# Sparse attention and a two-layer MLP on one core: batches 2 to 7 loaded by casting DMAs, MLP chunks one after the other, attention steps placed by a written plan

## The chip, the core and the metric

One NeuronCore of a Trainium2 chip runs the whole program. Its engines are TensorE (PE, with PEld for weight loads), VectorE (DVE), ScalarE (ACT), GpSimd (POOL) and SyncE (SP, which here only issues DMAs). The metric is the device time of one execution in microseconds.

## What is computed

Eight batches with eight heads of 576 tokens and 64 features go through masked attention, and the result, 4608 tokens by 512 features, through a two-layer MLP with a squared ReLU. Heads 0 to 3 are local (a key is seen if it lies 0 to 31 positions back), heads 4 to 7 are strided (a key is seen if it is not later and has the same position modulo 32).

```python
scores = scale * np.matmul(q, k.transpose(0, 1, 3, 2))
rel = pos[:, None] - pos[None, :]
mask_local = (rel >= 0) & (rel < 32)
mask_strided = (rel >= 0) & (pos[None, :] % 32 == pos[:, None] % 32)
attn = softmax(np.where(masks, scores, -1e9))
x = np.matmul(attn, v)            # then to (4608, 512): heads side by side
h = x @ w_in                      # 512 x 2048
g = np.maximum(h, 0.0) ** 2
out = g @ w_out                   # 2048 x 512
```

## The kernel before

**Units.** A unit is a pair of heads of one batch. Unit u = 4b + p: p = 0, 1 are the local pairs of batch b, p = 2, 3 its strided pairs; so units 4 to 7 are batch 1, units 8 to 11 batch 2, and so on. A local unit has six blocks of 96 queries with 128 keys each, a strided unit eight blocks of 72 queries with 72 keys.

**Steps of a unit.** T (`step_T`, L270) transposes rows of q or k by six or eight PE transposes (L278) into a PSUM bank and copies it to SBUF on ACT (q, L291) or DVE (k, L293). S (`step_S`, L299) computes the scores (L327), four exponentials on ACT (L337, a half of one head each) and two mask products on DVE (L343); for units above 3 the exponentials and masks are handed out one per group by `later`. D (`step_D`, L385) multiplies with v (L405) in two or three parts and normalizes on DVE (L417, L418). E (`step_E`, L421) brings the result into `xt`, the MLP's input with features on partitions: by PE transposes (L435) and a copy (L441, L443), or, for local units from batch 2 on, by a DMA transpose (L428). For strided units of batch 0 the steps N and O (L359, L372) take the place of D and E: row sums by a product with ones, 1/sum by Ln and Exp on ACT, and the product with v straight in the layout of `xt`.

**Loads.** Batches 0 and 1 come largely by casting DMAs that POOL issues (float32 in HBM, bf16 in SBUF). From batch 2 on, SP loads float32 rows of q, k (L111, L117) and v (L191, L235), and POOL casts them: q and k on L139, local v on L198 and, for the 32 keys ahead of each block, L199, strided v on L242. Strided q and k go from HBM to HBM with a cast (L159) and are read back by a DMA transpose (L167). Local q and k of batches 2 and 3 are transposed on PE (`has_T`, L521, with LB = 4), those of batches 4 to 7 by DMA transposes on SP (L179).

**MLP.** The 4608 tokens form nine chunks of 512. Chunk c needs `xt` of all batches up to c (chunk 8 needs no more than batch 7). The first layer of a chunk has 16 groups (`mm1`, L451): four matmuls of 512 columns (L459) into one of the two banks "ph", ReLU on ACT (L465), square on DVE (L466). The second layer has 16 groups (`mm2`, L470): four matmuls (L480), four groups to a bank, then a copy on ACT (L484) and a store issued by SP (L488). There are 288 groups in one list, and PE executes in the order in which instructions were written.

**What sets the order.** Chunks 0, 1 and 2 have their first and second layers one after the other, with the second layer of chunk 2 and all later ones interleaved, group by group, with the first layer of the next chunk (L692 to L697); the second layer of chunk 8 stands alone at the end. Batch 0 is written out by hand (`first_steps`, L505), batch 1 too (`second`, L727 to L746, groups 12 to 31), and from batch 2 on `stream_steps` (L524) makes one list of steps, which is dealt out over the groups in proportion to weights (L750 to L757). Loads of a batch hang on a group too (`plan`, L706). In the first 32 groups three groups (`NP`) of chunk 0 are done piecewise while the last units of batch 0 finish.

Of the kernel before, what the change touches and what calls it, by code (L numbers as in the profile page):

```python
# [11 lines left out]
ALU = mybir.AluOpType  # L12

@with_exitstack
def kernel(
# [16 lines left out]
    QL = 96  # L32
# [10 lines left out]
    qkT = ctx.enter_context(tc.tile_pool(name="qkT", bufs=3))  # L43
# [28 lines left out]
    mask_loc = singles.tile([128, 1, QL], BF16)  # L72
    mask_str = singles.tile([SP_, 1, SP_], BF16)
# [3 lines left out]
    vl_sts = [singles.tile([128, 2 * NL, D], FP32, name=f"vl_st{i}") for i in range(2)]  # L77
# [13 lines left out]
    rv0 = b0[:, n_s:n_s + 4 * S].bitcast(FP32).rearrange("p (u c) -> p u c", u=2)  # L91
# [10 lines left out]
    LB = 4  # L102

    def load_qk_local(u, eng, gate=None):
        b, p = units[u]
        s = st.setdefault(u, {})
        for name, src in (("q", q), ("k", k)):
            t = qk_st.tile([QL, 2, 6 * D], FP32, name=f"{name}_st")
            if b >= LB:
                for hh in range(2):  # L110
                    eng.dma_start(out=t[:, hh].rearrange("p (t d) -> p t d", d=D),  # L111
                                  in_=src[b, 2 * p + hh].rearrange("(t p) d -> p t d", p=QL))
                s[name + "f"] = t
                continue
            if gate is not None and name == "q":
                nc.gpsimd.tensor_copy(t[0:1, 0, 0:1], gate)
            eng.dma_start(out=t, in_=src[b, 2 * p:2 * p + 2]  # L117
                          .rearrange("h (p j) d -> p h (j d)", j=6))
            s[name + "f"] = t

# [12 lines left out]
    def cast_qk_local(u, copies, names="qk"):  # L133
        s = st[u]
        for name, copy in zip("qk", copies):
            if name not in names:
                continue
            t = qk_in.tile([QL, 6, 2, D], BF16, name=f"{name}_l")
            copy(t.rearrange("p j h d -> p h j d"),  # L139
                 s[name + "f"].rearrange("p h (j d) -> p h j d", j=6))  # L140
            s[name] = t

    def load_qk_str(u):
        b, p = units[u]
        s = st.setdefault(u, {})
        for name, src in (("q", q), ("k", k)):
            t = strT.tile([128, NJ // 2, 4 * SP_], BF16, name=f"{name}T_s")
# [75 lines left out]
    def load_str_first(names):  # L223
        for i, (name, src) in enumerate((("q", q), ("k", k))):
            if name not in names:
                continue
# [572 lines left out]
```

## Time and profile before

| what | value |
| --- | --- |
| three runs | 321.79, 324.76 and 327.16 us, median 324.76 us |
| profiled execution | span 320.8 us, granted clock 0.999; no time of its own is recorded beside the span |
| matmuls of the first layer, L459 | 561 of 576 recorded |
| mean of one ReLU (L465), of one exponential (L337) | 597 ns, 406 ns |
| mean of one square (L466) | 486 ns |
| POOL casts and copies L139, L198, L199, L221, L242 | 820 to 1780 ns each |

The span runs from the first to the last instruction. In the chain of waits each piece is what the end of the program waited for at that moment; "issue" is time in which nothing visible was waited for. In a row of the timeline the first number is the start in microseconds, the second the duration, and the bracket says what the engine sat idle for.

### The profile page before, as it was taken

The numbers are of one execution on the slowest core, as the hardware profiler recorded it, in microseconds if no ns is written. First come the engines' busy times: TensorE is split into PE (matmuls) and PEld (weight loads), VectorE is DVE, ScalarE is ACT, GpSimd is POOL, SyncE is SP. The second block draws the span as 40 slices with busy tenths as digits, with TensorE's granted clock in tenths as the row PEclk, the third lists the DMA queues.
The fourth block names the chain that finished last, engine by engine and source line by source line (L and its number), as shares of the span: only waits on it lengthen the run. The fifth ranks groups of instructions, "written<-read, shape, count | busy, mean of one in ns | idle before, by whom it ended". The sixth has DMA issues, their size and how long they took to land.

```text
span 320.8 us, 6155 instructions
## 1 busy us (share of the span) xinstructions
PE 300.4 (94%) x2343; PEld 149.3 (47%) x2387; DVE 167.6 (52%) x406; ACT 162.3 (51%) x333; POOL 87.6 (27%) x110
## 2 busy tenths in 40 slices
PE   8779789999899989999999999999999999999995
PEld 3444345545455444444444444454454444444442
DVE  4465664467775886675576556555565222222200
ACT  3557554587454755554555455545543443444311
POOL 8653364707840822560092007000000000000000
PEclk9999999999999999999999999999999999999999
DMA  7999969799989999998697676000110110000121
GB/s 134 184 207 201 191 124 249 184 237 231 213 164 188 202 236 183 227 204 183 150 231 162 144 150 140 35 33 35 51 53 33 56 45 33 33 33 35 45 86 65
DMA packets 86444, 43.22 MB, mean 135 GB/s; under 512 B 70992, under 2 KB 79888, under 8 KB 86224
## 3 DMA queue, kind: packets, MB, share of 16 engines
q1 hardware_dynamic: 73520, 31.86, 46.2%
q0 software_dynamic: 12896, 10.98, 22.4%
q8 instruction: 18, 0.29, 0.4%
q14 instruction: 10, 0.08, 0.1%
HBM read 36.70 MB, written 12.98 MB: 155 GB/s over the span
## 4 chain that ended last, share of the span: by engine, by line
PE 83%; DVE 8%; issue 3%; ACT 3%; DMA 2%; POOL 0%; DVEq 0%; ACTq 0%; POOLq 0%
PE ph L459 36%; PE py L480 27%; PE ph L480 9%; PE pt L405 4%; PE pt L327 4%; DMA w_out_b<-in_k_dram 2%; DVE g_sb L466 2%; PE pt L435 2%; ACT r L465 1%; PE pt L278 1%; DVE xt L443 1%; DVE e L343 1%; DVE kTl L293 1%; DVE x_s L418 1%; PE pt L480 1%
## 5 line engine op out<-in xcount | busy, mean ns | idle before, releaser
L459 PE MATMUL ph<-xt,w_in_b 128*128 128x512 bf16 x557 | 142.8, 379 | 4.1 <-DVE xt L443 1.9
L465 ACT ACTIVATE r<-ph 128x512 bf16<-128x512 f32 x143 | 85.3, 597 | 99.9 <-PE ph L459 96.8
L466 DVE TENSOR_TENSOR g_sb<-r 128x512 bf16<-128x512 bf16 x144 | 69.7, 486 | 107.1 <-ACT r L465 106.7
L480 PE MATMUL py<-w_out_b,g_sb 128*128 128x512 bf16 x383 | 100.2, 379 | 1.3 <-issue 0.5
L480 PEld LDWEIGHTS <-g_sb 128*128 128x128 bf16 x576 | 52.7, 98 | 59.6 <-issue 3.1
L459 PEld LDWEIGHTS <-w_in_b 128*128 128x128 bf16 x576 | 51.8, 98 | 55.1 <-issue 2.0
L337 ACT ACTIVATE e<-pt 128x288 bf16<-128x288 f32 (+1 forms) x128 | 48.3, 406 | 15.7 <-PE pt L327 15.5
L480 PE MATMUL ph<-w_out_b,g_sb 128*128 128x512 bf16 x151 | 36.7, 379 | 0.7 <-issue 0.3
L405 PEld LDWEIGHTS <-e 72*128 72x128 bf16 (+1 forms) x416 | 22.2, 97 | 18.3 <-issue 1.7
L198 POOL CAST vl<-vl_st 128x768 bf16<-128x768 f32 x12 | 11.3, 938 | 54.4 <-PE ph L459 19.1
L418 DVE TENSOR_TENSOR x_s<-pt,rinv 72x384 bf16<-72x384 f32 (+1 forms) x42 | 21.4, 509 | 1.4
L417 DVE RECIPROCAL rinv<-pt 96x6 f32<-96x6 f32 (+2 forms) x74 | 13.6, 184 | 11.2 <-PE pt L405 9.3
L418 DVE TENSOR_TENSOR x_l<-pt,rinv 96x384 bf16<-96x384 f32 x32 | 17.7, 554 | 1.1
L139 POOL CAST q_l<-q_st 96x768 bf16<-96x768 f32 x12 | 10.9, 909 | 24.3 <-DMA q_st<-in_q_dram 22.8
L343 DVE TENSOR_TENSOR e<-e,mask_str 72x576 bf16<-72x576 bf16 x28 | 15.9, 570 | 2.1 <-ACT e L337 2.1
L484 ACT COPY y<-py 128x512 f32<-128x512 f32 x25 | 14.6, 585 | 4.4 <-PE py L480 4.4
L405 PE MATMUL pt<-vs,e 72*128 72x65 bf16 x224 | 14.2, 193 | 1.6 <-ACT e L337 1.1
L343 DVE TENSOR_TENSOR e<-e,mask_loc 128x576 bf16<-128x576 bf16 x28 | 15.3, 547 | 0.0
L484 ACT COPY y<-ph 128x512 f32<-128x512 f32 x10 | 5.9, 585 | 17.1 <-PE ph L480 17.1
L242 POOL CAST vs<-v_st 72x1024 bf16<-72x1024 f32 x12 | 14.0, 1195 | 0.4
L139 POOL CAST k_l<-k_st 96x768 bf16<-96x768 f32 x12 | 10.6, 886 | 10.2 <-DMA k_st<-in_k_dram 10.2
L405 PE MATMUL pt<-vl,e 128*128 128x65 bf16 x192 | 10.7, 193 | 0.2 <-DVE e L343 0.2
(97 smaller groups left out, 165.5 us busy)
## 6 DMA issues: line engine op xcount, KB each, us to landing
out_dram<-y SPq DMA_DIRECT2D x36, 256.0 KB, 2.0
vl_st<-in_v_dram SPq DMA_DIRECT2D x24, 144.0 KB, 4.3
v_st<-in_v_dram SPq DMA_DIRECT2D x12, 288.0 KB
q_st<-in_q_dram SPq DMA_DIRECT2D x16, 144.0 KB, 3.9
k_st<-in_k_dram SPq DMA_DIRECT2D x16, 144.0 KB, 5.7
w_in_b<-in_moe_w_in_dram POOLq DMA_DIRECT2D x4, 512.0 KB, 13.4
w_out_b<-in_moe_w_out_dram POOLq DMA_DIRECT2D x4, 512.0 KB, 14.0
q_d<-in_q_dram POOLq DMA_DIRECT2D x6, 288.0 KB, 4.9
```

The source lines that it names most:

```text
L139: copy(t.rearrange("p j h d -> p h j d"), s[name + "f"].rearrange("p h (j d) -> p h j d", j=6))
L242: (copy or nc.gpsimd.tensor_copy)(t[:, :, 0:D], s["vf"].rearrange("p h (j d) -> p (h j) d", d=D))
L337: nc.scalar.activation(e[0:kn, lo:lo + S // 2], pss[row][half][0:kn, 0:S // 2], AF.Exp, scale=scale)
L343: nc.vector.tensor_tensor(x, x, m.to_broadcast([kn, n, w]), op=ALU.mult)
L405: nc.tensor.matmul(po[:, n - n0, :], e[0:kn, pos(n):pos(n) + 128], rhs[0:kn, src(n), 0:D + 1], start=True, stop=True)
L417: nc.vector.reciprocal(rinv[0:w, 0:m], po[0:w, 0:m, D:D + 1])
L418: nc.vector.tensor_tensor(x, po[0:w, 0:m, 0:D], rinv[0:w, 0:m].to_broadcast([w, m, D]), op=ALU.mult)
L459: nc.tensor.matmul(ph, w_in_b[:, kk, 128 * ff:128 * (ff + 1)], xt[kk][:, 512 * c:512 * (c + 1)], start=(kk == order[0]), stop=(kk == order ...
L465: nc.scalar.activation(r, ph, AF.Relu)
L466: later(1, lambda: nc.vector.tensor_tensor(g[:, ff, :], r, r, op=ALU.mult))
L480: nc.tensor.matmul(py, g[:, ff, 128 * j:128 * (j + 1)], w_out_b[:, ff, :], start=(ff == 0), stop=(ff == 15))
L484: nc.scalar.copy(y, py)
```

## The change

From batch 2 on, all rows of q, k and v come by casting DMAs that POOL issues; SP keeps the stores and the DMA transposes. Local q and k arrive as bf16 rows (two DMAs for a unit and tensor, one per head) and are transposed by DMA in all batches from 2 on. Local v arrives in one DMA per batch, which also brings the 32 keys ahead of each block. Strided v arrives as bf16 and is spread into its padded tile by DVE or ACT (step B). POOL keeps one copy of its own, the shift of batch 0's v (step H).

Strided q and k of batches 0 and 1 come as rows of 96 partitions and are transposed for both units at once (step W, `step_TS`); local units of batch 0 take N and O too. The mask of local scores is held for all six blocks.

From chunk 2 on the second layer of a chunk follows its first; the last 128 tokens are finished in two halves of 256 columns (`last_y`), copied by ACT and DVE and stored from two queues.

Every step is a word in BATCH0 or PLAN: a letter for the step, a unit or batch, and where it applies q or k, a part, and the engine that copies (a for ACT, v for DVE, g for POOL). The number ahead of a line is the group before which its words are written; chunk c's first layer is groups 32c to 32c + 15 and its second the 16 after. c is a cast from the staged rows, Q loads local rows, V and U load v, C and X are the cast in HBM and the transposed read of strided q and k, Y is the DMA transposes of a local unit, l and r are loads of batch 1, o is a quarter of w_out, z the late constants, P part of the first three groups. S with "!" writes the four exponentials at once.

```diff
+FIRST = (0, 2, 3, 1)
+NP = 3
+BATCH0 = """
+    c0qa T0qa c0kv w2 T0ka S0 W0k0v W0q0a c1kv W0k1a c1qv W0q1v T1qv T1kv S2 S3 N2 N3 S1 O3 N0 H0g O0 O2
+    N1 O1 P0 P23 P1
+"""
+PLAN = """
+2: l1q4+5 l1k4+5 r1q r1k o0 o1 U1
+3: z V1 o3 o2
+4: C2
+6: Q8q Q9k Q9q Q8k V2 U2
+8: c4qa W1q0v c4kv c5qv
+10: T4qa T4kv T5qa
+11: c5kv
+12: S4!
+13: T5ka
+15: W1q1a
+16: S5! W1k0v
+17: W1k1a
+18: S6 B6v
+19: S7
+20: B7v D4.0 D4.1
+21: D5.0
+22: X2 Y8
+23: D5.1 E4a
+24: D6.0 E5a D6.1
+25: Y9 D6.2 D7.0
+26: E6
+27: D7.1
+29: D7.2
+30: E7v
+33: C3
+35: Q12q
+36: Q13k
+38: Q13q Q12k V3
+39: U3
+40: S8!
+41: S9
+42: D8.0
+43: D8.1
+44: E8
+45: S10!
+46: D9.0 D9.1
+48: B10v
+49: S11! X3
+50: D10.0 D10.1
+51: E9
+52: D10.2
+54: B11v Y12 Y13 D11.0
+55: E10
+57: D11.1
+62: C4
+63: D11.2 Q17k Q17q
+64: E11v S12! Q16q
+66: Q16k V4
...
+121: D19.0
+124: D19.1 D19.2
+126: E19 V6
+127: Q25k
+129: S20!
+130: C6
+131: S21
+133: Q24q
+134: U6 Q25q D20.0 D20.1
+136: Q24k S22 E20
+139: D21.0
+140: D21.1 E21
+141: S23
+144: B22v
+146: D22.0
+147: X6 D22.1
+148: Y24 D22.2 B23v
+149: E22
+150: Y25
+153: D23.0
+155: D23.1
+156: D23.2
+158: E23 S24!
+160: Q28q
+161: S25 D24.0
+162: Q28k Q29k D24.1
+163: U7 C7 Q29q V7
...
+187: Y29 D27.2
+189: E27
+192: S28!
+193: S29
+195: D28.0 D28.1
+196: E28
...
+216: B31v
+217: D31.0
+219: D31.1
+220: D31.2
+223: E31v
+"""
...
+    mask_all = singles.tile([128, NL, QL], BF16)
...
-    vl_sts = [singles.tile([128, 2 * NL, D], FP32, name=f"vl_st{i}") for i in range(2)]
...
+    def load_qk_rows(u, name):
+        b, p = units[u]
+        src = q if name == "q" else k
+        t = qk_in.tile([QL, 6, 2, D], BF16, name=f"{name}_l")
+        for hh in range(2):
+            nc.gpsimd.dma_start(out=t[:, :, hh, :], in_=src[b, 2 * p + hh].rearrange("(t p) d -> p t d", p=QL))
+        st.setdefault(u, {})[name] = t

...
+    def load_str_rows(b, name):
+        src = q if name == "q" else k
+        if b == 0:
+            c = 4 if name == "q" else 8
+            t = w_out_b[0:QL, c:c + NP3, :]
+        else:
+            t = xt[1 if name == "q" else 2][0:QL, T - NP3 * 512:T].rearrange("p (s c) -> p s c", s=NP3)
+        nc.gpsimd.dma_start(out=t, in_=src[b, 4:8].rearrange("h (p j) d -> (h p) (j d)", j=NJ)
+                            .rearrange("(s p) c -> p s c", p=QL))
+        str_rows[b, name] = t
+
+    def step_TS(b, name, g, copy):
+        src = str_rows[b, name]
+        pt = bank("ph" if b == 0 else "pt").bitcast(BF16)[:, 0:S]
+        for i in range(2):
+            for s3 in range(NP3):
+                c = 128 * (2 * g + i)
+                o = S // 2 * i + QL * s3
+                nc.tensor.transpose(pt[:, o:o + QL], src[:, s3, c:c + 128], ident[0:QL, 0:QL])
+        if g == 0:
+            str_T[b, name] = strT.tile([128, NJ // 2, 4 * SP_], BF16, name=f"{name}T_s")
+        o = str_T[b, name]
+        copy(o[:, 2 * g:2 * g + 2, :].rearrange("c a r -> c (a r)"), pt)
+        if g == 1:
+            for i in range(2):
+                st.setdefault(4 * b + 2 + i, {})[name + "T"] = o[:, :, 2 * SP_ * i:2 * SP_ * (i + 1)]
+
...
+    def load_v_str(b):
+        t = v_st.tile([SP_, 4, NJ * D], BF16, name="v_st")
...
+    def spread_v_str(u, copy):
+        t = vss[v_slot(u)]
+        copy(t[:, :, 0:D], st[u]["vf"].rearrange("p h (j d) -> p (h j) d", d=D))
+        st[u]["v"] = t
...
+    def load_v_local_all(b):
+        i = (2 * b) % NV
+        t = vl_all[:, i:i + 2]
+        src = v[b - 1:b + 1].rearrange("b h s d -> (b h s) d")
+        r0 = H * S - 32
+        src = bass.AP(src.tensor, src.offset + r0 * D, [[D, 128], [QL * D, 4 * NL], [1, D]])
+        nc.gpsimd.dma_start(out=t[:, :, :, :, 0:D].rearrange("p u h t d -> p (u h t) d"), in_=src)
+        for u in range(2):
+            st.setdefault(4 * b + u, {})["v"] = t[:, u]
...
-            m = mask_loc if local else mask_str
-            nc.vector.tensor_tensor(x, x, m.to_broadcast([kn, n, w]), op=ALU.mult)
+            m = mask_all if local else mask_str.to_broadcast([kn, n, w])
+            nc.vector.tensor_tensor(x, x, m, op=ALU.mult)
...
+        if mode == 1:
+            for row in range(2):
+                for half in range(2):
+                    expo(row, half)
+                later(row + 1, lambda row=row: masks(row), u)
...
+            rv = rv0[:, u, hw * half:hw * (half + 1)]
+            if is_local(u):
+                for t in range(NL // 2):
+                    for h in range(2):
+                        c = S * h + hw * half + QL * t
+                        nc.tensor.matmul(po[64 * h:64 * h + 64, QL * t:QL * (t + 1)],
+                                         vls[u][:, h, NL // 2 * half + t, 0:D], e[:, c:c + QL],
+                                         start=True, stop=True)
+                nc.vector.tensor_tensor(xt[u][:, hw * half:hw * (half + 1)], po[:, 0:hw], rv, op=ALU.mult)
...
+    def last_y(c, j, i):
+        g, r0 = gs[c], 512 * c + 128 * j
+        if i == 0:
+            ys[c, j] = bank("py"), y_pool.tile([128, 512], FP32, name="y")
+        py, y = ys[c, j]
+        half, part = divmod(i, 2)
+        cols = slice(256 * half, 256 * (half + 1))
+        for ff in range(8 * part, 8 * part + 8):
+            nc.tensor.matmul(py[:, cols], g[:, ff, 128 * j:128 * (j + 1)], w_out_b[:, ff, cols],
+                             start=(ff == 0), stop=(ff == 15))
+        if part == 1:
+            (V if half else A)(y[:, cols], py[:, cols])
+            (nc.scalar if half else nc.sync).dma_start(out=out[r0:r0 + 128, cols], in_=y[:, cols])

...
+    def late_constants():
+        nc.vector.tensor_copy(mask_all, mask_loc.to_broadcast([128, NL, QL]))
+        nc.vector.memset(mask_all[0:32, 0], 0.0)
...
-    mm1_alone(2)
-    for c in range(3, NCH):
+    for c in range(2, NCH):
         for i in range(16):
             add(c, 1, i)
-            add(c - 1, 2, i)
-    for i in range(16):
-        add(NCH - 1, 2, i, "ph")
...
     for n, g in enumerate(groups):
-        while done < due[n]:
-            steps[done]()
-            done += 1
-        for fn in hooks.get(n, ()):
-            fn()
+        for word in plan.get(n, ()):
+            run_step(word)
         g()
         tick()
```

## The prediction

> **What bounds the kernel now.** I read the page's engine shares and its chain first, then the busy time of four stretches, then the chain of one steady stretch, and last the instructions that the chain names off PE.
>
> ```profile
> span 320.8 us, 6155 instructions
> PE 300.4 (94%) x2343; PEld 149.3 (47%) x2387; DVE 167.6 (52%) x406; ACT 162.3 (51%) x333; POOL 87.6 (27%) x110
> PE 83%; DVE 8%; issue 3%; ACT 3%; DMA 2%; POOL 0%; DVEq 0%; ACTq 0%; POOLq 0%
> ```
>
> PE is the bound; 17% of the end's chain runs through something else, mostly DVE. Only that and PE's own work can be saved.
>
> ```profile
> core 0: us, PE busy (x) PEld busy (x) DVE busy (x) ACT busy (x) POOL busy (x), PEclk, DMA share, GB/s
> 0.00:25.20 25.20, 19.93 (x232) 10.73 (x237) 12.57 (x37) 12.63 (x29) 15.97 (x27) 1.00 1.18 176
> 25.20:62.44 37.24, 32.46 (x307) 17.21 (x312) 22.78 (x60) 20.50 (x42) 18.36 (x23) 1.00 1.07 190
> 62.44:316.88 254.44, 248.06 (x1806) 121.37 (x1839) 132.26 (x310) 128.58 (x263) 53.26 (x61) 1.00 0.59 124
> 316.88:320.80 3.92, 0.00 (x0) 0.00 (x0) 0.00 (x0) 0.58 (x1) 0.00 (x0) 0.94 0.17 67
> ```
>
> The cuts are: 25.20, when groups begin to follow each other; 62.44, the first group of chunk 1 (group 32); 316.88, the end of the last matmul. I call them A, B, C, D. The clock is 1.00 throughout, so no clock term enters.
>
> ```profile
> 152.67 0.38 PE ph L459
> 157.73 0.40 PE pt L327 x16
> 158.13 0.97 PE ph L459 x4
> 159.96 0.86 PE ph L459 x4
> 160.83 0.18 PE pt L405 x6
> 173.42 0.36 PE pt L327 x12
> 175.61 0.26 PE pt L435 x8
> ...
> 184.04 0.77 DVE xt L443
> 184.85 0.38 PE ph L459
> ```
>
> This is the chain in the steady stretch. A group takes 0.864 us; a local S 0.36, a strided S 0.40, a part of D 0.18 (the short third one 0.12), a strided E 0.26. So a batch from 2 on costs PE 2 x (0.36 + 0.36) + 2 x (0.40 + 0.48 + 0.26) = 3.72. Chunks 4 and 5 begin at 152.67 and 184.85: 32.18 for 32 groups (27.65) and about a batch, so a batch costs 4.53 there: 0.77 is the copy into `xt` that the next first layer waits for, the rest short bubbles.
>
> ```profile
> L466 DVE TENSOR_TENSOR g_sb<-r x144: 354/425/1673, 25.2 to 302.9; 128x512 bf16<-128x512 bf16 x144
> ...
> 78.10 0.82 POOL L139 CAST k_l<-k_st 96x768 bf16<-96x768 f32 x1
> 78.87 0.82 POOL L198 CAST vl<-vl_st 128x768 bf16<-128x768 f32 x1
> ...
> 78.30 1.67 DVE L466 TENSOR_TENSOR g_sb<-r 128x512 bf16<-128x512 bf16 x1 [0.83 <-ACT r L465]
> 79.89 0.97 DVE L343 TENSOR_TENSOR e<-e,mask_str 72x576 bf16<-72x576 bf16 x1
> ```
>
> A square has a median of 0.425 and this one takes 1.67: it starts while POOL casts and ends after the casts. Taking all squares and mask products that overlap a POOL cast or copy, their time above the median adds up to 14.6 us; those that overlap only a DMA that POOL issues add nothing (8 of them, excess below 0.02). The chain crosses four such places: 36.50 (1.50), 42.20 (two masks, 1.76), 78.30 and 79.97.
>
> **The change part by part.** *POOL's casts go (from batch 1 on).* That frees DVE of nearly all of the 14.6 us, of which the end feels only what lies on the chain. DVE gets the spreads of strided v (B): 14 less one on ACT, near 0.35 x 1024/768 = 0.46 each from the copy of 96x768 bf16 (0.35), 6 us in all, against 14.6 less; hidden beside PE, since DVE is at 52%.
>
> *Loads by POOL's queue.* A batch issues eight Q, one V, one U and two C: 8 x 0.69 + about 1.3 + 0.73 + 2 x 0.49 = 8.5 us of POOL (rows L149, L214, L207, L159), where casts and C took 11.5. SP loses its loads and keeps 2 X, 4 Y, 2 E and four stores, 8 x 1.3 + 4 x 0.35 = 11.8 us in 32. Neither queue is full; what waits behind a late DMA on SP are E's transposes and the stores. A batch's casting loads are 4608 rows of q and k and 3072 of v, 256 bytes read and 128 written. The trace's packet records give such rows a median of 32 ns against 18 for 256-byte rows without a cast: 7680 x 32 / 16 engines = 15.4 us per batch where batches 4 to 7 took 6912 x 25 (mean) / 16 = 10.8. The DMA share in C is 0.59, and after 200 us nearly nothing is loaded, so I take zero; the plan puts Q8 to Q9 at group 6 and their transposes at 22 and 25, 16 us or more, where loads landed in 13 to 15 us at the busiest. Bounds: 0, and 3 us a batch (rival 3).
>
> By the Trainium skill, page "DMA: Bandwidth & Descriptors", section Specifications, a transfer needs 512 bytes or more for line rate, and below that DMA reads, modifies and writes: that speaks against 128-byte rows. It states no factor; if it doubled the 15.4 us, about 43 us of DMA would stand against 31 us per batch, and the sum would be some 70 us higher, an estimate. The trace disagrees as far as it goes: 70992 of 86444 packets are under 512 bytes already, and PE waits for no load after 10 us.
>
> *Transposes.* In batches 2 and 3 eight T of 0.26 (the row of six L278 in the chain) leave PE: -2.1, and with them copies on ACT (0.64) and DVE (0.75). W of batches 0 and 1 replaces T of strided units at the same four banks per batch and six transposes for eight: 0. Y on SP is hidden; it lands in about 4 us.
>
> *Stage A.* Strided k is issued after the identity, at 2.9 and not 3.82, and its landing at 10.15 is what the chain waits for. But W needs four copies before the first strided S, so that one begins near 11.7 (11.18 before). Then ACT is the chain: S2 and S3 1.33 each, N2 and N3 1.39 each, S1 1.29, N0 and N1 1.39 each, 9.5 us from about 12.1 to 21.6; DVE has four products of 2 x 0.64, the last ending near 24.1; three matmuls of 0.216: 24.8. I take -0.4; bounds -2 (if DVE keeps up with ACT) and +2 (each N and O in series).
>
> *Stage B.* Groups 3 to 31 are 29 x 0.864 = 25.1; batch 1 costs 3.72 + 2 E and 8 T or W at 0.26 = 6.3. So 5.9 of 37.24 are waits: 1.77 at 36.96 and 0.76 at 41.5 for the copy of kT, where T sits one group before S; about 0.9 for masks behind POOL's copies; the rest under 0.5 each. The plan has T4 two groups before S4, POOL copies no more. I take half, -3.0; bounds -5.9 and +1 (late rows of r1q stall PE in order; W1q0 stands at group 8, near 29.5, and by the packet rate its rows land near 29).
>
> *Stage C.* 256 groups are 221.2 whatever their order. With every batch at the steady 4.53, six are 27.2, together 248.4. What is new: a first layer alone leaves ACT 0.864 for a ReLU of 0.60, and S now stands mostly there. Groups 128 to 143 hold S20 to S23: ACT 16 x 0.60 + 16 x 0.41 = 16.1, PE 13.8 + 0.8 + 0.7 + 0.7 = 16.0. Two banks ahead give ACT 0.26 of slack per group. Before, chunk 1's first layer held three S (67.6 to 76.1) with ACT 14.21 of 17.98 busy, and no wait in its chain is PE on the ReLU's bank. I take 0.25 a batch, 1.5; bounds 0 and one exponential for each of 24 S, 9.8. C becomes 249.9, -4.5 (the -2.1 of T is in it).
>
> *Stage D.* The last copy is half as wide (0.585 for 512 columns, so about 0.3) and its store half as long: -0.4; bounds -1.2 and 0. The full mask and `qkT`'s fourth buffer: 0, DVE time beside PE.
>
> **Sum:** 24.8 + 34.2 + 249.9 + 3.5 = 312.4 for a span of 320.8: -8.4. The span lies 1.0 under the fastest run and 3.9 under the median of 324.76; I add the 3.9: 316.3.
>
> **The rivals.** *1, more of the waits go:* B near its floor (32.0), C at 245.5 (3.72 and 0.33 of bubbles a batch), so 305.8 + 3.9 = 309.7. For it: no POOL cast is left to hold DVE, and E stands one group ahead of the chunk that needs it. Against: the bubbles after S are there without POOL. *2, ACT becomes the bound of the first layers alone:* 0.41 for each of 24 S, 8.3 above my 1.5: 324.6, no change. For it: 16.1 against 16.0. Against: chunk 1. *3, slower:* the rows that S needs land late. Everything goes through POOL's one queue in order, and S in PE's queue waits with all groups behind it. The point from which it decides is a delay beyond the 16 us between Q and Y; 3 us more for each of six batches is 18: 334. For it: 15.4 against 10.8 and 14 us landings in the first 40 us. Against: in C such landings are 3 to 6 us.
>
> **How the numbers follow.** Likeliest 0.50 at 316.3, its own range 312 to 321; rival 1 0.18, rival 2 0.18, rival 3 0.14. The range 308 to 328 leaves out rival 3 and a small tail below. A run tells about 2% from no change, 318.3 and 331.3. Below 318.3: rival 1 and three quarters of the likeliest, 0.18 + 0.38 = 0.56. Above 331.3: most of rival 3, 0.12. Between: 0.32.
>
> **What would show it.** Squares with a maximum near 0.45 and no excess; POOL with DMA issues and one copy; first layers of 15 to 16.5 us with S inside and no PE wait on ReLU above 0.5; group 32 near 59; last matmul near 309. I am wrong if the chain names a DMA into q_l, vl or kT after 30 us, or "ACT r" repeatedly between matmuls of first layers, or if the squares stay slow beside POOL's DMA issues.

## The result, and the profile after

The changed kernel takes 340.06 us (median of 4 runs, 338.87 to 342.12) where the kernel before took 324.52 in the same comparison (321.79 to 327.16): a ratio of 1.0505, 95% interval 1.043 to 1.0579. That is 5% slower, where 316.3 was forecast and 328.0 was the upper end of the range. The profiled execution took 338.87 us. Over all comparisons some runs of the kernel before are longer at a lower mean clock (324.5 to 329.6 us against 319.5 to 324.6), and the ratios of the experiments leave such runs out.

The first lines of the page of the changed kernel, engine shares and chain:

```profile
span 336.9 us, 5946 instructions
PE 306.4 (91%) x2288; PEld 151.8 (45%) x2326; DVE 154.6 (46%) x410; ACT 162.4 (48%) x338; POOL 72.7 (22%) x102
PE 58%; DMA 32%; SPq 3%; issue 3%; POOL 3%; DVE 1%; ACT 0%; POOLq 0%; DVEq 0%
```

209 instructions fewer and 13 us less of DVE, as the change intends; but DMA holds 32% of the chain, where it held 2%. The same four stretches as in the prediction, cut at the same events:

```profile
core 0: us, PE busy (x) PEld busy (x) DVE busy (x) ACT busy (x) POOL busy (x), PEclk, DMA share, GB/s
0.00:27.61 27.61, 22.56 (x214) 11.51 (x216) 10.21 (x30) 16.06 (x36) 17.68 (x29) 0.75 1.20 185
27.61:59.50 31.89, 31.62 (x299) 17.04 (x304) 21.55 (x63) 20.53 (x43) 13.81 (x19) 1.00 1.59 190
59.50:333.66 274.16, 252.26 (x1777) 123.27 (x1807) 122.40 (x317) 125.84 (x260) 41.19 (x54) 0.96 0.78 97
333.66:336.90 3.24, 0.00 (x0) 0.00 (x0) 0.42 (x1) 0.00 (x0) 0.00 (x0) 0.94 0.12 40
```

Against 25.20, 37.24, 254.44 and 3.92 before: A is 2.4 us longer, B 5.3 shorter, C 19.7 longer, D 0.7 shorter, 16.1 in all. Two things in the last columns are new: a granted clock of 0.75 in A and of 0.96 in C, where it was 1.00. What PE waits for, the longest entry of its waits (us in total, times, longest):

```profile
PE pt L458 <- DMA kTl<-k_l: 18.7, 4, 8.0
```

Line 458 is the score matmul of a local unit; `kTl<-k_l` is the transpose of its k by DMA, issued by SP (the step Y). In PE's timeline, round the second of the four waits, the brackets give the idle time and what ended it:

```profile
99.41 1.89 PE L608 MATMUL ph<-xt,w_in_b 128*128 128x512 bf16 x8
105.79 0.42 PE L458 MATMUL pt<-qT,kTl 64*128 64x96 bf16 x6 [4.48 <-DMA kTl<-k_l]
```

And the stretches round it:

```profile
102.00:106.00 4.00, 0.21 (x6) 0.22 (x8) 0.41 (x2) 0.00 (x0) 0.00 (x0) 0.80 1.46 234
106.00:110.00 4.00, 4.00 (x24) 1.37 (x20) 1.25 (x3) 1.92 (x5) 0.00 (x0) 0.50 0.05 12
```

Up to 106 PE stands nearly still while the DMA share is 1.46, and then it works from 106 to 110 without a break at clock 0.50: the wait is paid once as idle time and again as slow matmuls. The trace's clock records have four such spells in C (94.14 to 97.55, 104.38 to 111.21, 172.65 to 179.47, 210.19 to 213.61), each beginning within one of the four waits (92.20, 101.30, 167.81, 206.90). PE is busy for 14.4 us of their 20.5, so about half of that, 7.2 us, is lost to them, an estimate. C without the waits and without the slow clock would be 274.2 - 18.7 - 7.2 = 248.3.

Why the transposes are late is seen in their landings, from issue to landed, of the kernel before (three landings are recorded, of eight transposes) and then of the changed one (all twelve):

```profile
DMA to landing us min/median/max: 3.5/4.2/4.6
```

```profile
DMA to landing us min/median/max: 2.4/8.3/15.5
```

The fastest is faster than any of those three, the median is twice theirs, and the slowest took 15.5 (the wait at 101.30). What was in the way is suggested by the times at which POOL issues the casts of strided q and k from HBM to HBM (step C), here those of the kernel before for q of batches 3 to 5:

```profile
62.59 0.49 POOL L159 DMA_DIRECT2D q_d<-in_q_dram  x1
...
85.67 0.49 POOL L159 DMA_DIRECT2D q_d<-in_q_dram  x1
...
111.97 0.49 POOL L159 DMA_DIRECT2D q_d<-in_q_dram  x1
```

and those of the changed kernel for batches 3 to 6:

```profile
52.01 0.53 POOL L326 DMA_DIRECT2D q_d<-in_q_dram  x1
...
67.56 0.53 POOL L326 DMA_DIRECT2D q_d<-in_q_dram  x1
...
85.41 0.52 POOL L326 DMA_DIRECT2D q_d<-in_q_dram  x1 [0.48 <-DMA q_l<-in_q_dram]
...
149.37 0.52 POOL L326 DMA_DIRECT2D q_d<-in_q_dram  x1
```

Before, they come 23 and 26 us apart (the next two at 137.84 and 166.05), about a batch's time. After, three come within 33 us, and then none for 64. The plan has C5 at group 97, which PE reaches near 137; POOL issues it at 85.41, because on POOL's own queue nothing stands in front of it. What POOL waited for before, and after (us in total, times, longest):

```profile
POOL q_l L139 <- DMA q_st<-in_q_dram: 22.8, 7, 10.6
POOL vl L198 <- PE ph L459: 19.1, 1, 19.1
POOL vl L198 <- DMA vl_st<-in_v_dram: 19.1, 4, 10.5
POOL vl L198 <- PE py L480: 15.3, 1, 15.3
```

```profile
POOL vl L383 <- PE pt L554: 43.6, 3, 26.0
POOL v_st L356 <- DVE vs L362: 23.9, 2, 18.9
```

L139 and L198 are the casts that the change removes. They waited for loads to land (two of L198's waits, 19.1 and 15.3 us, end by the profile with a matmul of PE), and so held back each issue behind them. The loads that they waited for stood on SP's queue, among stores that waited in their turn:

```profile
SPq L488 <- ACT y L484: 83.0, 16, 7.3
```

After, all loads are on POOL's queue, and the longest times for which it is held are those in which a buffer is still in use: it loads two batches in a rush and then stands.

### The profile page after: what moved, and what is told of

Read it like the earlier page. It is cut to its first block, busy times and chain, and to the rows that moved or that the text cites. A ratio compares the mean times of both kernels' runs of the same rounds, so it can differ in the third digit from the quotient of the medians.

```text
span 336.9 us, 5946 instructions
## 1 busy us (share of the span) xinstructions
PE 306.4 (91%) x2288; PEld 151.8 (45%) x2326; DVE 154.6 (46%) x410; ACT 162.4 (48%) x338; POOL 72.7 (22%) x102
## 3 DMA queue, kind: packets, MB, share of 16 engines
HBM read 38.08 MB, written 12.98 MB: 152 GB/s over the span
## 4 chain that ended last, share of the span: by engine, by line
PE 58%; DMA 32%; SPq 3%; issue 3%; POOL 3%; DVE 1%; ACT 0%; POOLq 0%; DVEq 0%
PE ph L608 28%; PE ph L630 23%; DMA kTl<-k_l 11%; DMA q_l<-in_q_dram 6%; DMA w_out_b<-in_moe_w_out_dram 5%; DMA vl<-in_v_dram 5%; DMA k_st<-in_k_dram 4%; PE pt L458 3%; SPq L346 3%; PE pt L554 2%; PE py L652 1%; PE pt L584 1%; POOL k_l L268 0%; POOL q_st L279 0%; POOL vl L383 0%
## 5 line engine op out<-in xcount | busy, mean ns | idle before, releaser
L630 PE MATMUL ph<-w_out_b,g_sb 128*128 128x512 bf16 x511 | 122.0, 382 | 1.0 <-issue 0.2
L615 DVE TENSOR_TENSOR g_sb<-r 128x512 bf16<-128x512 bf16 x144 | 60.4, 423 | 77.3 <-ACT r L614 75.5
L608 PEld LDWEIGHTS <-w_in_b 128*128 128x128 bf16 x576 | 54.4, 100 | 64.1 <-issue 8.4
L634 ACT COPY y<-ph 128x512 f32<-128x512 f32 x33 | 19.3, 586 | 88.7 <-PE ph L630 88.3
L468 ACT ACTIVATE e<-pt 128x288 bf16<-128x288 f32 (+1 forms) x128 | 46.2, 408 | 24.8 <-PE pt L458 24.7
L566 DVE RECIPROCAL rinv<-pt 96x6 f32<-96x6 f32 (+2 forms) x70 | 12.9, 185 | 36.0 <-PE pt L554 35.3
L458 PE MATMUL pt<-qT,kTl 64*128 64x96 bf16 x192 | 8.7, 226 | 19.3 <-DMA kTl<-k_l 18.7
L554 PEld LDWEIGHTS <-e 128*128 128x128 bf16 (+1 forms) x392 | 19.7, 97 | 13.7 <-DVE e L474 0.3
L474 DVE TENSOR_TENSOR e<-e,mask_all 128x576 bf16<-128x576 bf16 x28 | 12.7, 453 | 24.7 <-ACT e L468 24.3
L268 POOL DMA_DIRECT2D q_l<-in_q_dram x24 | 17.6, 738 | 26.8 <-DMA qT<-q_l 10.6
L383 POOL DMA_DIRECT2D vl<-in_v_dram x7 | 10.1, 1438 | 46.9 <-PE pt L554 43.6
L268 POOL DMA_DIRECT2D k_l<-in_k_dram x24 | 17.5, 734 | 10.5 <-DMA k_l<-in_k_dram 3.7
L567 DVE TENSOR_TENSOR x_l<-pt,rinv 96x384 bf16<-96x384 f32 x28 | 15.5, 554 | 1.0
L592 DVE COPY xt<-pt 128x576 bf16<-128x576 bf16 x11 | 8.3, 758 | 10.2 <-PE pt L584 10.2
## 6 DMA issues: line engine op xcount, KB each, us to landing
w_in_b<-in_moe_w_in_dram POOLq DMA_DIRECT2D x4, 512.0 KB, 11.9
v_st<-in_v_dram POOLq DMA_DIRECT2D x7, 288.0 KB, 10.9
q_d<-in_q_dram POOLq DMA_DIRECT2D x6, 288.0 KB, 12.7
```

The lines of the kernel that those rows point to most:

```text
L268: nc.gpsimd.dma_start(out=t[:, :, hh, :], in_=src[b, 2 * p + hh].rearrange("(t p) d -> p t d", p=QL))
L458: nc.tensor.matmul(pss[row][half][0:kn, w * i:w * (i + 1)], lhsT, rhs, start=u > 3, stop=True, skip_group_check=u < 4)
L468: nc.scalar.activation(e[0:kn, lo:lo + S // 2], pss[row][half][0:kn, 0:S // 2], AF.Exp, scale=scale)
L474: nc.vector.tensor_tensor(x, x, m, op=ALU.mult)
L554: nc.tensor.matmul(po[:, n - n0, :], e[0:kn, pos(n):pos(n) + 128], rhs[0:kn, src(n), 0:D + 1], start=True, stop=True)
L566: nc.vector.reciprocal(rinv[0:w, 0:m], po[0:w, 0:m, D:D + 1])
```

## The experiments

All kernels below run beside the kernel before. "Wait" is PE's on `kTl<-k_l`, "landing" its median and longest; "group 32" is the start of that group's ReLU and "last" the end of the last matmul in the profiled execution, so their difference is stage C without its first 1.1 us. The median of the kernel before was 321.8 to 324.6 us in these comparisons.

| kernel | us (median) | ratio to before, 95% interval | wait | landing | group 32 | last | C |
|---|---|---|---|---|---|---|---|
| before | | | 0 | 4.2 / 4.6 | 63.50 | 316.87 | 253.4 |
| changed | 340.06 | 1.0505 (1.043 to 1.0579) | 18.7 | 8.3 / 15.5 | 60.62 | 333.65 | 273.0 |
| b_cp | 324.47 | 1.0109 (1.005 to 1.0167) | 0 | | 66.24 | 319.04 | 252.8 |
| a_cp | 325.21 | 1.0138 (1.0055 to 1.022) | 8.3 | 7.6 / 12.3 | 60.60 | 320.74 | 260.1 |
| a_cp_gate | 313.55 | 0.9775 (0.9726 to 0.9824) | 0 | 2.9 / 8.0 | 60.62 | 307.76 | 247.1 |
| a_cp_warm | 329.06 (324.31 to 330.89) | 1.0173 (1.0054 to 1.0293) | 11.9 | 7.6 / 11.9 | 58.30 | 322.71 | 264.4 |
| a_cp_gate_warm | 311.26 | 0.9671 (0.9602 to 0.9739) | 0 | 2.5 / 8.0 | 58.30 | 305.44 | 247.1 |
| a_cp_gateC | 313.76 | 0.9699 (0.9614 to 0.9785) | 0 | 3.3 / 7.2 | 59.88 | 307.72 | 247.8 |
| a_cp_noC | 315.23 | 0.9795 (0.9728 to 0.9862) | 1.3 | 6.4 / 7.8 | 60.60 | 309.29 | 248.7 |
| a_cp_big | 319.56 | 0.9932 (0.989 to 0.9974) | 5.0 | 6.7 / 10.9 | 60.63 | 313.55 | 252.9 |
| a_cp_early | 322.88 | 1.0037 (0.9995 to 1.0078) | 0 | 7.0 / 9.5 | 60.58 | 317.40 | 256.8 |
| a_cp_C1k | 325.14 | 1.0113 (0.9998 to 1.0228) | 6.9 | 8.3 / 10.2 | 60.61 | 319.26 | 258.7 |
| a_cp_gate_casts | 319.95 | 0.9937 (0.9894 to 0.998) | 0.8 | 2.9 / 7.1 | 61.50 | 314.28 | 252.8 |

**First round: the DMA transposes replaced by PE.** In a_pe and b_pe PE transposes everything that DMA transposed in batches 2 to 7.

```
-            Y: nc.sync.dma_start_transpose(...), X: the same, E of local units: the same
+            T, W, E on PE from batch 2 on          (b_pe: LB = 8, XB = 8)
```

> The changed kernel without any DMA transpose: local q and k of batches 2 to 7 are transposed on PE two to three groups ahead of their scores; strided q and k are still cast in HBM, read back as plain rows and transposed on PE (step W); local results go into xt by PE. All casting loads of POOL stay where the plan has them. PE gets 4 + 4 + 2 sets of transposes of 0.26 us per batch, 15.6 us in six batches. Theory 1 (only the DMA transposes were late, the casting loads are in time, and the order of chunks costs nothing): no PE wait on a DMA above 1 us after 30 us, clock 1.00 from 30 us on, span 336.9 - 18.7 (the four waits) - 7 (slow clock behind them) + 15.6 = 327, time 326 to 333. Rival A (casting rows come too late): PE waits for q_l, k_l or vl, above 336. Rival B (first layers alone are bound by ACT): no DMA waits, first layers above 18 us, time above 336.

> The kernel before without any DMA transpose (both of its batch bounds for transposes set to 8): local and strided q and k of all batches and all local results are transposed on PE, all else is as it was, POOL casts included. PE gets 4.2 + 6.2 + 3.1 = 13.5 us of transposes more than before, so 338, with 335 to 343 for the copies on ACT and DVE. Theory 1 (the rest of the change is worth about what was forecast): the changed kernel in the same form is 6 to 11 us faster than this. Rival (the rest of the change is worth nothing or costs time): the two are within 3 us.

Measured: a_pe 340.38 us (ratio 1.0528, 1.0446 to 1.0609), b_pe 360.01 (1.115, 1.1042 to 1.1258). Both above what was expected: a_pe has 9.4 us of PE gaps on ACT and DVE after 27.6 us, b_pe 21.2 us of gaps on DVE and four spells of half clock. What it tells: no DMA wait in a_pe after 30 us, and the changed kernel is 20 us faster than the one before (6 to 11 expected) when neither has a DMA transpose. As a measure of the change it is poor, since PE gains work. By its signs a_pe came out as its rival B: no wait for a DMA, above 336 us, and most of its first layers over 18 us, up to 20.1. What speaks against that rival for the change itself is a_cp_gate below, whose first layers, with PE's work left as it is, take 12.9 to 15.8 us from their first ReLU to their last.

In a_px only the local q and k of batches 2 to 7 are moved by SP again, as plain copies of as many bytes (their transposition is left out); a_px_gate holds POOL at the plan's lines.

```
+        if n >= 33 and any(w[0] in "CQVU" for w in plan.get(n, ())):
+            nc.vector.memset(toks[:, i, 0:1], 0.0)
+            nc.gpsimd.tensor_copy(seen[:, i, 0:1], toks[:, i, 0:1])
         for word in plan.get(n, ()):
             run_step(word)
```

> As the changed kernel without DMA transposes, but local q and k of batches 2 to 7 go from their rows to their place in S by plain DMAs of the same bytes on SP's queue, at the places in the plan where the transposes stood (two DMAs per tensor, 768 pieces of 192 bytes, where the transpose had 576 packets of 256). This leaves out their transposition, so the scores of these units are of other data; it shows what any DMA at that place meets. Theory 1, general (casting loads that POOL issues crowd the DMA engines): these copies land 7 to 15 us after their issue in batches 3 to 6, and PE waits for kTl 8 to 19 us in all; time 330 to 345. Rival (only transposes suffer so): landings of 3 to 5 us, waits under 3 us, time 6 below the variant with PE transposes, 320 to 327.

> As the variant with plain copies in place of the transposes, but POOL is held at every plan line that loads (from group 33 on) until DVE has come to that line (a tiny memset on DVE, a tiny copy on POOL per line), so that loads do not run ahead of the plan; the transposition of local q and k of batches 2 to 7 is left out as there. Theory 1a (loads issued 10 to 50 us ahead of the plan are what crowds the copies): landings of 3 to 6 us, waits for kTl under 4 us, 320 to 328. Rival (loads crowd the copies at their planned times as well, or come too late when held): waits as without the hold, or waits on q_l, k_l, vl, above 330.

Measured: a_px 341.45 us (1.057) with 5.5 us of waits on `kTl<-k_l`; a_px_gate 334.75 (1.037, 1.0272 to 1.0467) with none. The landings of a_px, then of a_px_gate:

```profile
DMA to landing us min/median/max: 1.9/5.9/11.1
```

```profile
DMA to landing us min/median/max: 1.9/2.3/5.9
```

The same copies land in less than half the time, in the median, when POOL is kept to the plan, and the kernel is 6.7 us faster for a wait of 5.5. The spells of half clock don't explain the rest: after 30 us the profile of a_px has one, that of a_px_gate two. The waits of a_px are below the 8 to 19 us expected, and the level of a_px_gate missed its 320 to 328, as in a_pe, by PE's added work.

**Second round: PE's work left as it is.** Now copies of as many bytes on SP's queue stand in for every DMA transpose (Y, X and E of local units; the transposition is left out from batch 2 on), in the kernel before (b_cp) and in the changed one (a_cp).

```
-            nc.sync.dma_start_transpose(out=dst.rearrange("c (t p) -> c t p", p=QL),
-                                        in_=s[name].rearrange("p t h d -> p (t h d)"))
+            row = s[name].rearrange("p t h d -> p t (h d)")[:, :, 0:QL]
+            nc.sync.dma_start(out=to[0:QL], in_=row)
+            nc.sync.dma_start(out=to[QL:128], in_=row[0:128 - QL])
```

> The kernel before, in which plain copies of the same bytes on SP's queue stand in for all DMA transposes (q and k of batches 4 to 7, strided q and k and the local outputs of batches 2 to 7), so that the transposition itself is left out there and PE's work is that of the kernel before. It is the base for the three runs beside it. Theory: the landings that PE waits for were hidden before and stay so, 318 to 325 us. Rival (landings of the transposes cost the kernel before something that its chain doesn't show): under 316.

> The changed kernel with the same stand-ins (it leaves the transpositions of batches 2 to 7 out). Theory (copies on SP's queue land late because the casting loads crowd them, PE stands and is then clocked down): kTl<-k_l lands in a median of 5 to 8 us, PE waits 5 to 18 us for it, 325 to 337 us, slower than the base beside it. Rival (only the DMA's own transposing is slow, the loads don't matter): landings of 2 to 3 us, no wait, 310 to 318 us, faster than the base.

> As the run before it, and from group 33 on POOL is held at each line of the plan that loads, until DVE has come to that line: one element written by DVE, read by POOL. Theory (POOL runs ahead of the plan and its loads fall on the copies): landings near 2.3 us, no PE wait on kTl, no half clock after 30 us, so the order of the change shows what it is worth without the waits: 336.9 less 18.7 of waits, 7.4 of half clock = 311 span, 310 to 318 us. Rival A (the order itself is the loss): waits gone and still 325 or more. Rival B (held loads come late): PE waits for q_l or vl instead, 325 or more.

b_cp behaves as the kernel before (C 252.8 against 253.4). a_cp has the change's trouble in a milder form: it is 12 us above a_cp_gate. The landings and the longest wait of PE in a_cp:

```profile
DMA to landing us min/median/max: 1.9/7.6/12.3
PE pt L462 <- DMA kTl<-k_l: 8.3, 5, 3.7
```

The landings and the two longest waits in a_cp_gate:

```profile
DMA to landing us min/median/max: 1.9/2.9/8.0
PE py L667 <- DVE xt L743: 1.3, 1, 1.3
PE ph L310 <- DMA w_out_b<-in_k_dram: 0.8, 1, 0.8
```

and stages B and C of a_cp_gate:

```profile
27.61:59.50 31.89, 31.63 (x300) 17.04 (x305) 21.16 (x63) 20.51 (x43) 9.80 (x13) 1.00 1.52 196
59.50:308.00 248.50, 245.51 (x1777) 121.14 (x1807) 122.31 (x342) 125.05 (x260) 50.41 (x84) 1.00 0.69 107
```

B is that of the changed kernel (31.63 us of PE for 31.62), with the cut ahead of it at the same time; C ends at 307.76 and lasts 248.3 us instead of 274.2, at clock 1.00. That is the 248.3 worked out above (the expectation had taken 7.4 us for the slow clock). With nothing late the change is worth what was hoped for (313.55 against b_cp's 324.47 from the same comparison); the landings take it away.

**The head's clock.** The change leaves ten filling matmuls of nineteen (the expectation says sixteen: the trace has records of so many of the nineteen).

```
-    c0qa T0qa c0kv w2 T0ka S0 W0k0v ... N2 N3 S1 O3
+    c0qa T0qa c0kv w2 T0ka w3 S0 w5 W0k0v ... N2 w1 N3 S1 w1 O3      (and w1 twice more)
```

> As a_cp, and 12 more filling matmuls in the first 22 us (22 in all; the kernel before has 16, the changed one 10). Theory (the head lost its clock because the change has fewer fillers): clock 1.00 from 12 to 26 us, group 3 at 24.5 to 25.5 instead of 27.6, 2 to 3 us less than a_cp. Rival (the half clock of the head comes by chance of the run or from the waits for rows): the clock is 0.50 there all the same, no change or up to 1 us more.

> As a_cp_gate, with the 12 more filling matmuls of a_cp_warm. Theory (in a_cp_warm the head gained 2.3 us and the waits for landings gave it back, since PE then asks for them earlier): with POOL held there is nothing to give back, clock 1.00 from 6 us to the end, 2 to 2.5 us below a_cp_gate, 310 to 312 us. Rival (an earlier PE runs into new waits for held loads): waits on q_l, vl or kTl above 1 us, no gain, 313 or more.

Eight microseconds of the head of the changed kernel, and the same of a_cp_warm:

```profile
12.00:16.00 4.00, 4.00 (x45) 2.17 (x44) 1.18 (x2) 2.49 (x8) 3.45 (x5) 0.53 1.24 207
16.00:20.00 4.00, 3.82 (x42) 1.70 (x39) 0.77 (x2) 3.94 (x12) 1.33 (x3) 0.50 1.25 206
```

```profile
12.00:16.00 4.00, 3.75 (x56) 2.04 (x55) 1.42 (x2) 3.15 (x10) 3.23 (x5) 1.00 1.25 209
16.00:20.00 4.00, 3.26 (x66) 1.87 (x66) 1.20 (x2) 3.90 (x12) 1.61 (x3) 1.00 1.24 204
```

With 22 fillers the clock stays at 1.00 here and group 32 starts at 58.30 and not 60.60: 2.3 us, as expected. In a_cp_warm it doesn't reach the end: PE asks for the copies earlier, the waits grow from 8.3 to 11.9 us (one of 7.1), and the kernel is not faster. With POOL held it does reach it: 311.26 us, 2.3 below a_cp_gate, clock 1.00 to the end. The fillers are not the whole cause: b_cp, with the nineteen of the kernel before, ran its head at 0.50 from 10.82 to 21.06, and the profiled execution of the kernel before did not:

```profile
12.00:16.00 4.00, 4.00 (x49) 2.59 (x49) 1.45 (x4) 1.73 (x6) 1.24 (x2) 0.50 1.37 203
16.00:20.00 4.00, 3.78 (x29) 1.80 (x30) 1.51 (x2) 2.61 (x7) 3.25 (x5) 0.50 1.23 204
```

Which of the two the same head gets seems to change from run to run. The kernel before shows it in its own times: beside a_cp_gateC, ten of its 19 runs have a mean clock of 0.997 or more and take 320.12 to 323.94 us, and seven have 0.976 to 0.982 and take 325.23 to 327.12 (that the loss is in the head is shown for b_cp's profile alone). The profiles of the two kernels with 22 have no slow clock in the head after 6.3 us, but of the four runs of a_cp_gate_warm two have a mean clock below 1.00 (0.995 and 0.989), so that many fillers don't make it certain.

**Which loads are in the way.** In a_cp_noC the casts from HBM to HBM of batches 3 to 7 are left out; in a_cp_big local q and k are written in pieces of 768 bytes instead of 128, in another order.

```
-            nc.gpsimd.dma_start(out=t[:, :, hh, :], in_=src[b, 2 * p + hh].rearrange("(t p) d -> p t d", p=QL))
+            nc.gpsimd.dma_start(out=row[:, 6 * D * hh:6 * D * (hh + 1)],
+                                in_=src[b, 2 * p + hh].rearrange("(p j) d -> p (j d)", j=6))
```

> As a_cp, without the casts of the strided q and k from HBM to HBM in batches 3 to 7 (batch 2's are read again in their place; no gate). Theory (all loads in POOL's queue crowd the copies, the 128-byte rows of q, k and v the most): kTl<-k_l still lands in 5 us or more, waits of 3 to 8 us, 319 to 325 us. Rival (the 18-KB packets of these casts are what holds the engines): median landing under 4 us, waits under 2, 312 to 317 us.

> As a_cp, with the casting loads of local q and k written in pieces of 768 bytes (six rows of a head one after the other per partition, so the order of the rows is left out too) instead of 128; no gate. 27648 packets of 32 ns, 55 us of 16 engines, become 4608 of about 80, 23 us. Theory (the small rows make the crowd): landings of kTl<-k_l under 5 us in the median, waits under 3, 313 to 318 us. Rival (any load that POOL issues ahead crowds them, whatever its rows): landings of 6 to 8, waits of 5 or more, 320 to 326 us.

I had put the small rows first; a_cp_noC came out as the rival in time and waits, though not in the median landing. Without those casts the median landing is still 6.4, but nothing takes longer than 7.8, and of the waits 1.3 us are left. With large rows the waits are 5.0 and the time is halfway, 319.56; 3.3 us of that are shorter waits, and no spell of half clock falls into C. So each part of the traffic adds, and the casts from HBM to HBM (without those of five batches HBM reads fall from 41.62 to 35.72 MB and writes from 12.98 to 10.03) are what lifts a landing beyond the slack between Y and S, which from batch 3 on is 9 to 15 groups of 0.86 us, 8 to 13 us, and 6 groups for Y29.

**Their packets, or when they come.** An 18-KB packet of these casts has a median of 1.38 us in the trace's packet records. a_cp_Csmall was to cut them, but neighbouring pieces were joined again (the packet counts are those of a_cp), so it is only a second measurement of a_cp: 327.39 us, 1.0124 (1.007 to 1.0177). a_cp_C1k changes the order of the target's rows, so that they can't be joined.

```
-                out=t.rearrange("(x y) c -> x (y c)", x=16),
+                out=t.rearrange("(a b) c -> b a c", a=16),
```

> As a_cp, with the casts of strided q and k from HBM to HBM in 288 pieces of 1 KB instead of 16 of 18 KB (same bytes, same place in POOL's queue, no gate). Theory (an 18-KB packet holds its DMA engine 1.4 us and more, and what queues behind such packets lands late): kTl<-k_l lands in at most 9 us, waits under 3, 314 to 318 us, as without these casts. Rival (their traffic from HBM to HBM is what costs, whatever the size): landings up to 11 or 12 us, waits of 6 or more, 322 to 327 us.

> As a_cp_Csmall was meant (its packets stayed at 18432 bytes, since neighbouring pieces were joined): the casts of strided q and k from HBM to HBM with the order of the target's rows changed, so that pieces of 1 KB can't be joined. Theory (an 18-KB packet holds its DMA engine 1.4 us and more): no packet of 18432 bytes, kTl<-k_l at most 9 us, waits under 3, 314 to 318 us. Rival (their traffic at that moment is what costs, whatever the size): waits of 6 or more, 322 to 328 us.

> As a_cp, with POOL held (until DVE has come to the line) only ahead of the five casts from HBM to HBM of batches 3 to 7; the loads between them still run ahead. Theory (it is these casts, 40 and more groups ahead of their place, that fall on the copies): waits under 2, 313 to 317 us. Rival (any load that runs ahead is as bad): waits of 5 or more, 320 to 326 us.

> As a_cp, with the copies of local q and k of batches 3 to 7 named 7 to 16 groups (6 to 14 us) earlier in the plan, nothing held. Theory (what counts is the slack between a copy's issue and its use against a landing of up to 12 us): landings stay at 6 to 12 us, waits fall under 3, 314 to 318 us. Rival (a copy named earlier stands behind its own casting load on SP's queue, and the stores behind it): no fewer waits, 322 us or more.

The packets of a_cp and of a_cp_C1k:

```profile
DMA packets 109644, 38.01 MB, mean 117 GB/s; under 512 B 95600, under 2 KB 104944, under 8 KB 109424
```

```profile
DMA packets 115596, 38.02 MB, mean 118 GB/s; under 512 B 98288, under 2 KB 111088, under 8 KB 115568
```

220 packets of 8 KB and more became 28, and the time stayed: 325.14 against 325.21, waits of 6.9 us. The size of the packets is not the cause; my theory fell there. By the Trainium skill, page "DMA: Bandwidth & Descriptors", section Queues, rings and completion order, a DMA engine takes turns between the queues packet by packet, and a packet there typically holds 9 to 17 descriptors. From that I had inferred that long packets keep another queue's transfer waiting; this pair of runs shows no such effect, and no run here shows the turns themselves.

a_cp_gateC holds POOL at five places only, ahead of these casts, and is as fast as a_cp_gate (313.76 and 313.55). That doesn't single out the casts: whatever stands behind one in POOL's queue is held with it, and the loads of batch 3 begin at 62.3 us in a_cp_gateC, at 64.1 in a_cp_gate and at 51.9 in a_cp. What the two show is that it matters when POOL's queue issues. a_cp_early names the copies 7 to 15 groups earlier and lets POOL run. The waits on kTl are gone, but the longest of PE is now another one:

```profile
PE ph L614 <- DMA xt<-x_l: 6.8, 1, 6.8
```

It begins at 93.02, where a_cp waits for kTl at 92.43. A transfer behind the copies on SP's queue, the output of unit 9 (step E), is issued at 86.58 instead of 77.25 in a_cp, because the copies now stand ahead of it, and lands after 13.0 us instead of 10.0. 322.88 us, 2.3 less than a_cp (4.5 less than a_cp_Csmall, which ran beside it); my theory had said 314 to 318, and the rival, which named SP's queue, 322 or more. More slack for one transfer moves the wait to the next; taking the crowd away ends it.

**The relief of DVE.** a_cp_gate_casts puts casts on POOL that nobody reads.

```
+            for _ in range({"Q": 1, "V": 4, "U": 2}.get(word[0], 0) if n >= 33 else 0):
+                nc.gpsimd.tensor_copy(low, high)
```

> As a_cp_gate, with casts on POOL that nobody reads (96x768, fp32 to bf16, ten per batch from batch 3 on, each behind the load that it was with in the kernel before). It puts back what DVE was relieved of. Theory (DVE's two-input products are held while POOL casts, and part of the gain is this relief): mean square 450 to 490 ns instead of 423, 2 to 5 us above a_cp_gate, 315 to 319 us. Rival (DVE is at 49% and its relief is hidden behind PE): squares slow all the same, 313 to 314.5 us.

The squares on DVE of a_cp_gate, then of a_cp_gate_casts (busy us, mean ns, idle before):

```profile
L620 DVE TENSOR_TENSOR g_sb<-r 128x512 bf16<-128x512 bf16 x144 | 60.4, 423 | 71.3 <-ACT r L619 69.6
```

```profile
L620 DVE TENSOR_TENSOR g_sb<-r 128x512 bf16<-128x512 bf16 x144 | 71.1, 507 | 56.1 <-ACT r L619 55.2
```

The squares are slow again, and the time rises by 6.4 us, of which C has 5.6. The rest is in the head, where none of these casts stands but the slow clock lasted 17.1 us instead of 13.7. After 59.5 us PE's waits on DVE rise from 0.2 to 3.5 us, and waits for transfers are 0.8. DVE at 49% is not hidden: the relief is a real part of the gain, and even the 5.6 are above the 2 to 5 us that I had expected. With the casts back, C (252.8) is no shorter than in b_cp (252.8), so in C the new order of the chunks by itself shows no gain. The casts stand closer together here than in the kernel before, so they may cost less there.

## Why the prediction was wrong, step by step

| stage | before | forecast | changed | a_cp_gate | a_cp_gate_warm |
|---|---|---|---|---|---|
| A | 25.2 | 24.8 | 27.6 | 27.6 | 25.3 |
| B | 37.2 | 34.2 | 31.9 | 31.9 | 31.9 |
| C | 254.4 | 249.9 | 274.2 | 248.3 | 248.3 |
| D | 3.9 | 3.5 | 3.2 | 3.5 | 3.5 |
| span | 320.8 | 312.4 | 336.9 | 311.3 | 309.0 |

**The step that failed** is the one that cost the loads at nothing ("so I take zero") together with "Y on SP is hidden; it lands in about 4 us". The 4 us came from three recorded landings, in a trace in which POOL's casts paced the loads: I counted those casts as removed work, and not as what held POOL to the plan. With them gone the transposes landed in 8.3 us in the median and up to 15.5, where the plan leaves them 5 to 13. I compared the 16 us between Q and Y with landings of 14, and never the few groups between Y and S. That is 18.7 us of waits. What I had priced, the rows themselves, held: those of 128 bytes took a median of 32 ns in the changed kernel too. It is when they are issued that I left out. (The 43 us of DMA per batch for doubled rows, which the sum doesn't use, don't follow from the rows beside them: with the share of 0.59 it would be about 39.)

**No clock term.** "The clock is 1.00 throughout, so no clock term enters" was read from the trace of before and carried to a kernel whose PE stands still. The waits cost some 7.2 us more in C by it, and the head 2.3. By the Trainium skill, page "TensorE: Matmul & The Clock Gate", Part 1, an idle window of some 3.4 us halves the clock and a busy one of that length restores it. The runs agree in the spells, 3.41 us long or whole multiples of that; they differ in the gaps. In a_px_gate one of 2.00 us, and later two of 0.96 and 1.64 within 4.1 us, came with a spell (from 181.51 and from 208.82), while one of 2.51 (a_cp_big) did not. A wait need not be 3.4 us long to cost the clock.

**Rival 3** had the place and nearly the size (334), with 0.14. It named POOL's one queue and late rows in PE's order. What it missed is the second transfer: the rows come late (`q_l` holds 6% of the chain), and then SP's transposes of them, which share the 16 engines with that queue, come late as well (`kTl`, 11%). My argument against it, landings of 3 to 6 us in C, held for the pacing of before only. The sign named in advance, a DMA into kTl or q_l on the chain after 30 us, is there.

**What was right.** DVE's relief: mean square 486 to 423 ns, masks 570 and 547 to 447 and 453. B was undervalued: I took half of the 5.9 us of waits, and 5.3 went (31.9, rival 1's 32.0). How much of that is the relief and how much the plan's new places for T and W was not taken apart. C's steady price: 248.3 against 249.9 once nothing is late; the 1.5 us for ReLU in first layers alone did not come, since the waits of PE on `ACT r` sum to 0.3 us in a_cp_gate, and rival 2 with its 8.3 more is out. That 249.9 came so near is in part luck: it gave DVE's relief no gain of its own in C, and the last experiment finds up to 5.6 us there. D: 3.2 to 3.5 for 3.5. Without late landings and with a full clock in the head the sum would have been 3.4 us too high (309.0 for 312.4). The 3.9 us added for the median is no issue: the median is 3.2 above the span.

**What stays open.** The DMA transposes themselves were not varied: in every experiment copies or PE do their work. Real ones land later than copies in the same crowd (8.3 and 15.5 against 7.6 and 12.3), and why they do stays open. The 12.7 us between the profiled spans of the changed kernel and a_cp are more than covered by it: waits of 18.7 against 8.3, and some 7.2 against 3.5 lost to slow clock. That holding POOL would also mend the changed kernel with its real transposes is argued, from 274.2 - 18.7 - 7.2 = 248.3 and the 248.3 of a_cp_gate; it was not run.

## What to carry to other kernels

A queue that loses its computing instructions loses its pacing too: before you price what is removed from it, ask what each removed instruction waited for, and how far the queue will run ahead without it. Cost a transfer's landing by the traffic that the change will put beside it, not by the landing in the trace of before, and hold it against the slack of every consumer on every queue that shares the engines. If the loads run ahead, hold the loads; giving one late transfer more slack only moved the wait to the next.

## What the runs showed of the hardware

- A wait of PE costs more than its length. After the head, gaps of 2.99 us and above (up to 8.03) came with a spell of half clock in every profile here, seven of the ten between 2.0 and 2.61 us did (not 2.51 in a_cp_big and 2.00 in a_pe and a_px), and in a_px_gate two of 0.96 and 1.64 close together did; in the changed kernel 18.7 us of waits brought some 7.2 us lost to slow matmuls.
- The head's clock is not fixed by its instructions: with nineteen fillers one profiled execution ran it at 1.00 and another (b_cp) 10.24 us of it at 0.50, and its group 32 came 2.7 us later (66.24 against 63.50).
- Pieces that lie next to each other on both sides of a DMA are joined: 288 pieces of 1 KB went as 16 packets of 18432 bytes until the order of the rows was changed.
- With ten casts of 288 KB from HBM to HBM among the other loads, the longest landing of a copy of k (108 and 36 KB) on another queue was 12.3 us, or 10.2 where they went in pieces of 1 KB and not 18; without them it was 7.8.
